# Float32 for the first two blocks, six raw slots and another order of the first steps in a chunked-attention, mixing and FFN kernel

## The chip, the cores and the metric

The kernel runs on one core of a Trainium2 chip. The metric is device time in microseconds of one execution; the median of three runs stands for the kernel. Five engines have queues of their own: TensorE (PE, products; its weight loads are listed as PEld), VectorE (DVE), ScalarE (ACT), GpSimd (POOL) and SyncE (SP, which here issues nearly all transfers).

## The reference

Four batches of 768 tokens, 8 heads of 64. Each chunk of 32 queries sees 16 tokens to its left, itself, 8 to its right and 8 memory tokens. Then a gated mixing and an FFN follow:

```python
scores = scale * np.matmul(q_c, k_full.transpose(0, 1, 3, 2))
scores = scores - np.max(scores, axis=-1, keepdims=True)
a = np.exp(scores); a = a / (np.sum(a, axis=-1, keepdims=True) + 1e-09)
out[:, :, c_start:c_end] = np.matmul(a, v_full)
# mixing, x is the attention's output as (B, S, 512)
gate_pre += conv_w[k][None, None, :] * xp[:, k:k + S, :]      # 5 taps along the tokens
gate = 1.0 / (1.0 + np.exp(-gate_pre))
x = gate * (x @ w_val) @ w_out
# FFN on the normalised x
ch = np.maximum(xn @ w_ch1, 0.0) @ w_ch2                       # 512 -> 2048 -> 512
out = x + ch
```

The weights w_val, conv_w, w_out, w_ch1 and w_ch2 arrive as 64-bit floats, 20 pieces of 1 MB in all (and conv_w).

## The kernel before

**Tiling.** The tokens are cut into 24 sub-blocks of 128 (two pairs of chunks each). Sub-blocks are grouped into 13 blocks: one alone, eleven of two, one alone (lines 222 to 225). Each block goes through attention (`attention`, in 8 steps per sub-block), mixing (`mix`, 8 steps and 2 more per sub-block) and FFN (`ch1` and `ch2`, `finish`).

**Precision.** Nearly every product is made of three float16 products: both operands are scaled by a power of two and split into a high and a low half (`PASSES`, line 36). For the operands of attention, `attention` squares and sums q, k and v on ScalarE (lines 251 to 253), derives the scales with a small product and three integer operations (`totals`, `pow2`), and writes each high half on ScalarE and each low half on VectorE (lines 264 to 278, 320 and 321). The probabilities are turned around by two DMA transposes on SP's queue (line 325). Block 0 alone is mixed and sent through the FFN in float32, with unsplit weights (`split` is false for it); its attention is of the float16 kind.

**Weights.** `fetch` and `take` load a piece of a weight as raw 64-bit words; `to_f32` makes float32 of it with one ScalarE and one VectorE pass (lines 153 and 154). `gram` adds the products of the piece with itself to get a bound for its scale (line 197); ahead of them `fill` issues eight products of the preceding piece into a tile "idle" that nothing reads (lines 177 to 182). When all pieces of a weight are through, `weight_scale` gives its scale, and `split_weight` writes the two halves in place (lines 217 and 218). Raw pieces lie in four slots inside the tile of the second FFN weight, and, from the seventeenth piece on, mostly in two buffers of their own (line 160).

**Order.** Everything is cut into streams of steps: a (attention), x (mixing), f (FFN), w (fetches), m, 1 and 2 (conversion, scale and split of the mixing weights, the first and the second FFN weight), l (loads of q, k, v). The string `PLAN` (line 35) writes out the order of the first 126 steps; then `STEADY` (line 34) is gone through for each block, in which attention runs two blocks and mixing one block ahead of the FFN. The framework turns this order into the queues of the engines and may let an instruction pass another that waits. The loads of a sub-block use buffers that alternate between two (`NLD`).

Of the kernel before, what the change touches and what calls it, by code (L numbers as in the profile page):

```python
# [49 lines left out]
def chunk_attention_moe_kernel(ctx: ExitStack, tc: tile.TileContext,  # L50
# [39 lines left out]
    bd = [const.tile([P, HP, 2, 2, 2, CHUNK], F16, name=f"bd{i}") for i in range(2)]  # L90
# [149 lines left out]

    def attention(n, d, u):
# [51 lines left out]

        sc = at.tile([P, 2 * HP, NSEEN], F32, tag="sc", name="sc")
        by_group = sc.rearrange("p (a g) k -> p a g k", g=2)
        for g in range(2):
            for ch in range(2):
                pp = slice(ch * 64, (ch + 1) * 64)
                nc.scalar.activation(out=by_group[pp, :, g, :],  # L299
                                     in_=s_ps[g][pp, :, ch * CHUNK:ch * CHUNK + NSEEN], func=AF.Copy)  # L300
        wide = [P, 2 * HP, NSEEN]
        mx = sm_p.tile([P, 2 * HP, 1], F32, tag="mx", name="mx")
        nc.vector.tensor_reduce(out=mx, in_=sc, axis=AX.X, op=ALU.max)
        nc.vector.tensor_tensor(out=sc, in0=sc, in1=mx.to_broadcast(wide), op=ALU.subtract)
        nc.scalar.activation(out=sc, in_=sc, func=AF.Exp, scale=c_exp)

        if i == 0:
            nc.vector.memset(by_group[0:64, :, 0, 0:LEFT], 0.0)
        if i == NSUB - 1:
            nc.vector.memset(by_group[64:128, :, 1, NSEEN - RIGHT:NSEEN], 0.0)  # L310
        yield

        sm = sm_p.tile([P, 2 * HP, 1], F32, tag="sum", name="sum")
        rs = sm_p.tile([P, 2 * HP, 1], F32, tag="rs", name="rs")
        nc.vector.tensor_reduce(out=sm, in_=sc, axis=AX.X, op=ALU.add)
        nc.vector.tensor_scalar(out=sm, in0=sm, scalar1=1e-9, scalar2=2.0 ** -PSCALE, op0=ALU.add, op1=ALU.mult)
        nc.vector.reciprocal(out=rs, in_=sm)
        nc.vector.tensor_tensor(out=sc, in0=sc, in1=rs.to_broadcast(wide), op=ALU.mult)  # L318
# [12 lines left out]
        xT = d["xT"][:, :, u, :]  # L331
        if i == 0:
            nc.gpsimd.memset(xT[:, :, 0:KW - 1], 0.0)
        else:
            nc.gpsimd.tensor_copy(out=xT[:, :, 0:KW - 1], in_=tail[0][:, :, SUB:SUB + KW - 1])
        tail[0] = xT
# [10 lines left out]
        for g, t in enumerate(pv):  # L347
            for e in range(2):
                pp = slice(e * 64, (e + 1) * 64)
                o = xT[pp, :, c0 + g * 64:c0 + (g + 1) * 64].rearrange("p a (c q) -> p a c q", q=CHUNK)  # L350
                if e == 0 or n < EVAC_ACT:
                    nc.scalar.activation(out=o, in_=t[pp, :, :, e, :], func=AF.Copy, scale=c_pv[pp])
                else:
                    nc.vector.tensor_scalar(out=o, in0=t[pp, :, :, e, :], scalar1=c_pv[pp], scalar2=None,
                                            op0=ALU.mult)
        if d["split"]:
            xs = xT[:, :, c0:c0 + SUB]
            xh, xl = (t[:, :, off:off + SUB] for t in d["x"])
            nc.scalar.activation(out=xh, in_=xs, func=AF.Copy, scale=s[:, 2:3])  # L359
            nc.vector.scalar_tensor_tensor(out=xl, in0=xs, scalar=s[:, 2:3], in1=xh, op0=ALU.mult, op1=ALU.subtract)  # L360
# [5 lines left out]
    def open_block(j):  # L366
        d = blk[j] = {"T": blocks[j][1] * SUB, "iv": {}, "split": j > 0}
        d["xT"] = x_p.tile([P, HP, 2, KW - 1 + SUB], F32, tag="xT", name="xT")
        if d["split"]:
# [4 lines left out]

    def mix(j):
# [68 lines left out]
        for u in range(n):  # L444
# [255 lines left out]
```

## Time and profile before

| | us |
|---|---|
| median of 3 runs | 766.37 (765.82 to 766.48) |
| the profiled execution | 764.73 |
| its span, first to last instruction | 762.6 |
| PE busy | 724.4 (95%) |
| DVE busy | 529.5 (69%) |
| ACT busy | 423.4 (56%) |
| POOL busy | 8.9 (1%) |

The profile counts an engine as busy while one of its instructions runs; a chain of waits, a table of stages and a timeline can be drawn from the same trace. Because a product's end is modelled and products overlap, the time of a group of products is its busy time divided by their number, not the mean of one.

### The profile page before, as it was taken

What the parts mean: (1) busy time and instruction counts of PE and PEld (TensorE: products, weight loads), DVE (VectorE), ACT (ScalarE), POOL (GpSimd) and SP (SyncE); (2) the same over time, 40 slices, a digit from 0 to 9 for tenths busy, and PEclk for the clock granted to TensorE, in tenths of its full rate; (3) what the DMA queues carried; (4) which work ended last, traced back from release to release, by engine and by line L of the source; (5) the groups of instructions that cost most, each with busy time, mean ns of one, the idle gap of its engine ahead of it and who ended that gap; (6) DMA issues with size and microseconds to landing.
All of it is one profiled execution on the core that took longest, in us unless ns stands there. A gap on an engine that the chain in (4) does not pass through costs nothing.

```text
span 762.6 us, 15675 instructions
## 1 busy us (share of the span) xinstructions
PE 724.4 (95%) x6480; PEld 496.8 (65%) x6480; DVE 529.5 (69%) x1163; ACT 423.4 (56%) x733; POOL 8.9 (1%) x35
## 2 busy tenths in 40 slices
PE   3888988888999999999999999999999999999997
PEld 2457745655766766766766766766767766766675
DVE  5799988885865866866876776776776776662321
ACT  7879968764663663664564565465465464330210
POOL 2000000000000000000000000000000000000000
PEclk9999999999999999999999999999999999999999
DMA  9969433222232132232212223223223102010010
GB/s 355 358 223 341 181 90 91 78 77 70 63 77 71 63 77 70 68 72 70 77 64 70 77 64 81 66 70 82 59 77 91 43 18 53 16 26 30 1 43 15
DMA packets 69735, 68.93 MB, mean 90 GB/s; under 512 B 53280, under 2 KB 53280, under 8 KB 69664
## 3 DMA queue, kind: packets, MB, share of 16 engines
q1 hardware_dynamic: 69376, 67.91, 29.9%
q8 instruction: 51, 0.84, 0.5%
q14 instruction: 20, 0.16, 0.1%
q10 hardware_dynamic: 288, 0.02, 0.0%
HBM read 49.30 MB, written 6.29 MB: 73 GB/s over the span
## 4 chain that ended last, share of the span: by engine, by line
PE 77%; DVE 11%; ACT 7%; DMA 3%; issue 1%; ACTq 0%; DVEq 0%
PE c_ps L477 30%; PE acc L497 29%; PE yps L424 7%; PE val L406 7%; PE s_ps L287 3%; DVE gt L389 2%; PE pv L344 2%; DVE w L154 2%; DMA xn<-xh 1%; ACT bd L268 1%; ACT top L153 1%; DVE w L218 1%; DMA raw<-in_w_ch_dram 1%; ACT sc L299 1%; DMA pT<-p 1%
## 5 line engine op out<-in xcount | busy, mean ns | idle before, releaser
L497 PE MATMUL acc<-w,h 128*128 128x512 f16 (+1 forms) x1136 | 266.2, 385 | 0.0
L477 PE MATMUL c_ps<-xn,w 128*128 128x256 f16 (+1 forms) x2304 | 256.8, 269 | 6.7 <-DMA xn<-xh 6.7
L477 PEld LDWEIGHTS <-w 128*128 128x128 f16 x2304 | 216.1, 98 | 44.6 <-DMA xn<-xh 7.0
L497 PEld LDWEIGHTS <-h 128*128 128x128 f16 x1104 | 107.0, 98 | 114.8 <-DVE h L482 0.2
L480 ACT ACTIVATE h<-c_ps 128x512 f16<-128x512 f32 (+1 forms) x96 | 56.5, 589 | 79.0 <-PE c_ps L477 76.5
L482 DVE SCALAR_TENSOR_TENSOR h<-c_ps,h 128x512 f16<-128x512 f32 x92 | 63.0, 685 | 53.2 <-ACT h L480 53.2
L389 DVE SCALAR_TENSOR_TENSOR gt<-xT,cw_sb,gt 128x256 f32<-128x256 f32 (+1 forms) x208 | 82.4, 458 | 0.1
L424 PE MATMUL yps<-wo,hg 128*128 128x512 f16 x276 | 64.4, 383 | 0.0
L406 PE MATMUL val<-x,wv 128*128 128x256 f16 (+1 forms) x576 | 62.4, 268 | 0.9 <-ACT x L359 0.8
L406 PEld LDWEIGHTS <-wv 128*128 128x128 f16 x576 | 54.4, 98 | 7.3 <-issue 1.2
L299 ACT ACTIVATE sc<-s_ps 64x256 f32<-64x256 f32 x96 | 36.3, 378 | 24.5 <-PE s_ps L287 23.5
L253 ACT ACTIVATE vs<-vt 128x1024 bf16<-128x1024 f32 x24 | 25.1, 1047 | 38.6 <-PE pv L344 38.4
L424 PEld LDWEIGHTS <-hg 128*128 128x128 f16 x276 | 25.9, 98 | 29.1 <-issue 1.0
L457 ACT ACTIVATE xh<-xh 128x512 f16<-128x512 f32 x23 | 14.5, 629 | 47.3 <-DVE xh L446 25.8
L287 PEld LDWEIGHTS <-bd 128*128 128x128 f16 x576 | 28.4, 99 | 17.8 <-issue 13.6
L411 ACT ACTIVATE hg<-gt 128x512 f16<-128x512 f32 (+1 forms) x24 | 14.6, 611 | 44.7 <-DVE gt L408 44.7
L268 ACT ACTIVATE bd<-qt,s 64x512 f16<-64x512 f32 x48 | 34.2, 713 | 7.0 <-DVE s L123 5.6
L269 DVE SCALAR_TENSOR_TENSOR bd<-qt,s,bd 64x512 f16<-64x512 f32 x48 | 35.7, 745 | 2.0 <-ACT bd L268 0.7
L287 PE MATMUL s_ps<-ks,bd 128*128 128x96 f16 x576 | 30.2, 209 | 6.6 <-ACT ks L271 5.3
L458 DVE TENSOR_TENSOR xh<-xh,xh 128x512 f16<-128x512 f32 x23 | 15.9, 692 | 29.4 <-DMA xn<-xh 22.8
L504 DVE SCALAR_TENSOR_TENSOR y<-acc,co_w,y 128x512 f32<-128x512 f32 x23 | 16.2, 746 | 28.4 <-PE acc L497 28.4
L320 ACT ACTIVATE p<-sc 128x512 f16<-128x512 f32 x24 | 15.1, 627 | 37.4 <-DVE sc L318 37.4
(120 smaller groups left out, 778.2 us busy)
## 6 DMA issues: line engine op xcount, KB each, us to landing
vt<-in_v_dram SPq DMA_DIRECT2D x24, 512.0 KB, 4.3
kt<-in_k_dram SPq DMA_DIRECT2D x24, 384.0 KB, 3.7
w<-in_w_ch_dram SPq DMA_DIRECT2D x8, 1023.8 KB, 8.0
qt<-in_q_dram SPq DMA_DIRECT2D x24, 256.0 KB, 2.7
out_dram<-y SPq DMA_DIRECT2D x24, 256.0 KB, 2.1
w<-in_w_ch_dram SPq DMA_DIRECT2D x5, 1023.5 KB, 6.5
raw<-in_w_ch_dram SPq DMA_DIRECT2D x3, 1023.5 KB, 12.5
w<-in_w_val_dram SPq DMA_DIRECT2D x2, 1023.5 KB, 7.5
```

The costliest lines, as they stand in the source:

```text
L253: nc.scalar.activation(out=v2[0].bitcast(BF16), in_=vt, func=AF.Square, accum_out=ss[:, 2:3])
L268: nc.scalar.activation(out=hi, in_=src, func=AF.Copy, scale=s[pp, 0:1])
L269: nc.vector.scalar_tensor_tensor(out=lo, in0=src, scalar=s[pp, 0:1], in1=hi, op0=ALU.mult, op1=ALU.subtract)
L287: nc.tensor.matmul(out=t[:, hp, :], lhsT=bd[r0][:, hp, g].rearrange("p c e q -> p (c e q)"), rhs=k2[r1][:, hp, g, :], start=(x == 0), stop ...
L299: nc.scalar.activation(out=by_group[pp, :, g, :], in_=s_ps[g][pp, :, ch * CHUNK:ch * CHUNK + NSEEN], func=AF.Copy)
L389: nc.vector.scalar_tensor_tensor(out=o, in0=xT[:, hp, 0:n, kk:kk + SUB], scalar=cw_sb[:, kk, hp:hp + 1], in1=o, op0=ALU.mult, op1=ALU.add)
L406: nc.tensor.matmul(out=t[:, u, 0:T], lhsT=l, rhs=r, start=(x == 0), stop=(x == len(todo) - 1))
L424: nc.tensor.matmul(out=t, lhsT=l, rhs=r, start=(x == 0), stop=(x == len(todo) - 1))
L477: nc.tensor.matmul(out=t[:, u * T:(u + 1) * T], lhsT=l, rhs=r, start=(x == 0), stop=(x == len(todo) - 1))
L480: nc.scalar.activation(out=h[0], in_=t, func=AF.Relu)
L482: nc.vector.scalar_tensor_tensor(out=h[1], in0=t, scalar=0.0, in1=h[0], op0=ALU.max, op1=ALU.subtract)
L497: nc.tensor.matmul(out=a, lhsT=l, rhs=r, start=(m == 0 and x == 0), stop=(m == NM - 1 and x == len(todo) - 1))
```

## The change

- Attention of the first two blocks (three sub-blocks) goes through a new function `attention32`: the queries are copied unscaled into a float32 view of the tile that held both halves, the products take q, k, v and the probabilities in float32, and the probabilities are turned around by products with a unit matrix and moved out of PSUM by VectorE. It has 5 steps per sub-block. The tile of the queries is zeroed again before the first float16 attention.
- Mixing of both blocks is float32; the FFN is so for block 0 alone, as before.
- Raw pieces use six slots from the start: four in the second FFN weight's tile and two buffers.
- `fill` and its products go.
- `PLAN` is another order of 120 steps. A conversion whose piece has not been asked for asks for it.

The diff, without the code that only moved into `exponentials`, `normalize`, `place` and `activations`:

```diff
-NFILL = 8
+NF32 = 2
+FIRST = 1
-PLAN = "w2 a1 w2 a2 m2 w1 l1 a1 w1 m2 a4 m1 a1 w2 x2 1_1 x2 w1 1_2 w1 l1 1_1 w1 a2 1_1 w1 x1 a1 w1 x1 1_1 a1 x3 a1 1_1 a3 m4 a2 x1 1_1 2_1 a1 w1 1_1 w2 2_2 a1 2_1 w1 2_1 a1 w1 a2 2_1 x2 w1 x2 w1 x1 l1 x1 f2 x1 f1 x1 2_1 1_1 2_1 a4 f2 x3 2_1 f1 1_1 f1 2_1 f1 2_2 l1 2_2 1_6 2_1 x1 2_2 f1"
+PLAN = "l1 a2 w1 a1 w1 m1 a2 x2 m1 w2 x2 w1 m1 a3 w2 l1 w2 x1 m1 w1 x1 w1 x3 m1 1_2 a2 1_3 x1 1_1 w1 1_1 a2 w1 a3 x3 w1 x2 1_1 x2 m2 f1 w1 2_1 x1 f1 1_1 w1 2_1 x1 l1 x1 2_1 a2 x1 1_2 2_1 x1 a1 2_1 a1 2_2 1_1 2_1 f2 1_1 m1 w1 f1 l1 a1 l1 2_1 a1 1_1 f1 1_1 w1 f1 1_1 2_1 f2 2_4 a1 2_1 f1 2_1 1_1 2_1 m1"
...
-    bd = [const.tile([P, HP, 2, 2, 2, CHUNK], F16, name=f"bd{i}") for i in range(2)]
+    bdt = const.tile([P, 2, HP, 2, 2, 2, CHUNK], F16, name="bd")
+    bd = [bdt[:, r] for r in range(2)]
+    bd32 = bdt.rearrange("p r a g c e q -> p (r a g c e q)").bitcast(F32).rearrange(
+        "p (a g c e q) -> p a g c e q", a=HP, g=2, c=2, e=2)
...
-        at = 4 * (n % 4) + 1 if n < 16 else 13 if n == 18 else None
+        at = ([1, 5, 9, 13, None, None] * 2 + [1, 5, 9, 13, None, None, 13, None])[n]
...
-    idle = [None]
-
-    def fill(n):
-        if idle[0] is not None:
-            t = ps_c.tile([P, 512], F32, tag="c", name="idle")
-            for _ in range(n):
-                nc.tensor.matmul(out=t, lhsT=idle[0][:, 0:P], rhs=idle[0][:, 0:512], start=True, stop=True)
-        idle[0] = None
...
-        fill(NFILL)
-        if W is not W2:
-            idle[0] = w[:, :, 1]
...
+    first16 = sum(sizes[:NF32])
...
+    def attention32(n, d, u):
         b, i = divmod(n, NSUB)
         st = sub[n]
         qt, kt, vt = st["q"], st["k"], st["v"]
+        for e in range(2):
+            pp = slice(e * 64, (e + 1) * 64)
+            src = qt[pp].rearrange("p a (n q) -> p (a n) q", q=CHUNK)
+            dst = bd32[pp, :, :, :, e, :].rearrange("p a g c q -> p (a g c) q")
+            if e == 0:
+                nc.scalar.activation(out=dst, in_=src, func=AF.Copy)
+            else:
+                nc.vector.tensor_copy(out=dst, in_=src)
+        yield
+        s_ps = []
+        for g in range(2):
+            t = ps.tile([P, HP, KEYS], F32, tag="ps", name="s_ps")
+            for hp in range(HP):
+                nc.tensor.matmul(out=t[:, hp, :], lhsT=bd32[:, hp, g].rearrange("p c e q -> p (c e q)"),
+                                 rhs=kt[:, hp, g, :], start=True, stop=True)
+            s_ps.append(t)
+        yield
+        sc, by_group = exponentials(i, s_ps, float(D) ** -0.5)
+        yield
+        normalize(sc, 1.0)
+        t = ps.tile([P, HP, P], F32, tag="ps", name="pT_ps")
+        for hp in range(HP):
+            nc.tensor.matmul(out=t[:, hp, :], lhsT=sc[:, 2 * hp:2 * hp + 2, :].rearrange("p g k -> p (g k)"), rhs=eye,
+                             start=True, stop=True)
+        pT = at.tile([P, 2, HP, P], F16, tag="pT", name="pT").rearrange("p r a t -> p (r a t)").bitcast(F32)
+        pT = pT.rearrange("p (a t) -> p a t", a=HP)
+        nc.vector.tensor_copy(out=pT, in_=t)
+        yield
+        xT = place(d, u, i)
+        pv = [ps.tile([P, HP, 2, 2, CHUNK], F32, tag="ps", name="pv") for g in range(2)]
+        for hp in range(HP):
+            for ch in range(2):
+                for g in range(2):
+                    pp = slice(g * 64, (g + 1) * 64)
+                    nc.tensor.matmul(out=pv[g][:, hp, ch].rearrange("p e q -> p (e q)"),
+                                     lhsT=vt[pp, ch, hp * P:(hp + 1) * P], rhs=pT[pp, hp, ch * 64:(ch + 1) * 64],
+                                     start=True, stop=True)
+        activations(n, xT, pv, 1.0)
+        yield
+
+    def attention(n, d, u):
...
+        if d["f32"]:
+            yield from attention32(n, d, u)
+            return
+        if n == first16:
+            nc.gpsimd.memset(bdt, 0.0)
...
-        d = blk[j] = {"T": blocks[j][1] * SUB, "iv": {}, "split": j > 0}
+        d = blk[j] = {"T": blocks[j][1] * SUB, "iv": {}, "split": j > 0, "f32": j < NF32}
...
-        split = d["split"]
+        split = not d["f32"]
...
-                todo = [p for kc in range(KC) for p in passes(Wv.rows(kc, split, fc * P, P), [x[:, kc, 0:T] for x in d["x"]])]
+                todo = [p for kc in range(KC) for p in passes(Wv.rows(kc, split, fc * P, P), [x[:, kc, 0:T] for x in d["x"]]
+                                                           if split else [xT[:, kc, 0:n, KW - 1:KW - 1 + SUB]])]
...
-        for t in tops + bd + [eye]:
+        for t in (tops[0], bdt, *tops[1:], eye):
             nc.gpsimd.memset(t, 0.0)
...
             for jj in range(W.n):
+                while jj not in W.raw:
+                    next(streams["w"])
                 convert(W, jj)
...
-        per = {"a": lambda n: 8 * n, "x": lambda n: 8 + 2 * n, "f": lambda n: NM * n * SUB // 256}
+        per = {"a": lambda j, n: (5 if j < NF32 else 8) * n, "x": lambda j, n: 8 + 2 * n, "f": lambda j, n: NM * n * SUB // 256}
```

## Rows read from the trace of the kernel before

**Rows 1.** Engine totals of the page: busy time, share of the span, instructions.
```profile
PE 724.4 (95%) x6480; PEld 496.8 (65%) x6480; DVE 529.5 (69%) x1163; ACT 423.4 (56%) x733; POOL 8.9 (1%) x35
```
**Rows 2.** Stages: window, its length, then each engine's busy time; last columns named by the first line.
```profile
core 0: us, PE busy (x) PEld busy (x) DVE busy (x) ACT busy (x) POOL busy (x), PEclk, DMA share, GB/s
0.00:65.00 65.00, 45.40 (x423) 27.79 (x424) 50.56 (x111) 54.40 (x81) 4.99 (x14) 1.00 0.87 322
65.00:117.00 52.00, 46.43 (x413) 33.54 (x413) 48.97 (x103) 42.49 (x63) 0.31 (x2) 1.00 0.52 173
117.00:191.00 74.00, 64.90 (x604) 44.40 (x605) 57.52 (x114) 48.40 (x84) 0.59 (x3) 0.95 0.28 76
191.00:700.00 509.00, 509.00 (x4534) 351.12 (x4532) 357.87 (x805) 270.00 (x493) 2.97 (x16) 1.00 0.24 63
700.00:762.60 62.60, 58.65 (x514) 39.94 (x512) 14.54 (x32) 8.12 (x14) 0.00 (x0) 1.00 0.06 18
```
**Rows 3.** The same table for line 181 alone, first stage: PE, PEld, clock, DMA.
```profile
0.00:65.00 65.00, 24.29 (x96) 8.91 (x96) 1.00 0.87 322
```
**Rows 4.** Timeline of TensorE: start, duration, line, operation, count, idle before and its releaser.
```profile
13.86 1.03 PE L197 MATMUL gram<-wv 128*128 128x128 bf16 x8 [0.58 <-DVE wv L154]
17.00 0.62 PE L197 MATMUL gram<-wv 128*128 128x128 bf16 x8
...
64.77 3.17 PE L477 MATMUL c_ps<-xnf,w 128*128 128x128 f32 x26 [1.40 <-DVE xnf L452]
...
161.44 0.20 PE L344 MATMUL pv<-pT,vs 64*128 64x64 f16 x2 [2.05 <-DMA pT<-p]
```
**Rows 5.** Groups by form, 0 to 190 us, VectorE: busy, mean ns, idle before.
```profile
L154 DVE SCALAR_TENSOR_TENSOR w<-w,top 128x1024 int32<-128x1024 int32 x13 | 15.8, 1217 | 1.8 <-ACT top L153 1.8
L389 DVE SCALAR_TENSOR_TENSOR gt<-xT,cw_sb,gt 128x256 f32<-128x256 f32 x32 | 13.2, 475 | 0.0
L269 DVE SCALAR_TENSOR_TENSOR bd<-qt,s,bd 64x512 f16<-64x512 f32 x14 | 10.5, 747 | 1.5 <-ACT bd L268 0.7 <-issue 0.5
L277 DVE SCALAR_TENSOR_TENSOR vs<-vt,s,vs 128x1024 f16<-128x1024 f32 x7 | 9.0, 1283 | 0.4 <-ACT vs L276 0.4
L272 DVE SCALAR_TENSOR_TENSOR ks<-kt,s,ks 128x768 f16<-128x768 f32 x7 | 7.1, 1017 | 0.5 <-ACT ks L271 0.3
L321 DVE TENSOR_TENSOR p<-sc,p 128x512 f16<-128x512 f32 x7 | 4.8, 687 | 0.0
L360 DVE SCALAR_TENSOR_TENSOR x<-xT,s,x 128x512 f16<-128x512 f32 x5 | 3.7, 748 | 1.5 <-ACT x L359 1.5
L446 DVE TENSOR_SCALAR xh<-y,mv,rt 128x512 f32<-128x512 f32 x5 | 2.7, 546 | 0.2
L452 DVE TENSOR_TENSOR xnf<-xnT,g_sb 128x512 f32<-128x512 f32 x1 | 0.7, 684 | 0.0
```
**Rows 6.** The same view, ScalarE.
```profile
L253 ACT ACTIVATE vs<-vt 128x1024 bf16<-128x1024 f32 x9 | 9.4, 1047 | 2.6 <-PE pv L344 2.4 <-DMA vt<-in_v_dram 0.3
L276 ACT ACTIVATE vs<-vt,s 128x1024 f16<-128x1024 f32 x7 | 8.0, 1137 | 0.0
```
**Rows 7.** The same view, TensorE.
```profile
L477 PE MATMUL c_ps<-xnf,w 128*128 128x128 f32 x128 | 16.2, 279 | 1.4 <-DVE xnf L452 1.4
L497 PE MATMUL acc<-w,h 128*128 128x512 f32 x32 | 14.3, 595 | 0.0
L424 PE MATMUL yps<-wo,hg 128*128 128x512 f16 x48 | 12.1, 401 | 0.0
L406 PE MATMUL val<-x,wv 128*128 128x256 f16 x96 | 11.0, 272 | 0.9 <-ACT x L359 0.8
```
**Rows 8.** Timeline of TensorE, one sub-block's score and value products.
```profile
167.81 1.18 PE L287 MATMUL s_ps<-ks,bd 128*128 128x96 f16 x24
...
184.52 0.87 PE L344 MATMUL pv<-pT,vs 64*128 64x64 f16 x48
```
**Rows 9.** Chain that ended last, in order of time: start, duration, what.
```profile
75.30 5.62 DMA raw<-in_w_ch_dram
```
**Rows 10.** Stages as in rows 2, around one pause.
```profile
160.00:170.00 10.00, 8.23 (x95) 4.80 (x96) 8.86 (x18) 7.81 (x14) 0.00 (x0) 0.83 0.45 104
```

More of the change, by code (lines that the diff above doesn't have):

```diff
@@ new lines, in normalize, with place @@
+    def normalize(sc, by):
+        sm = sm_p.tile([P, 2 * HP, 1], F32, tag="sum", name="sum")
+        rs = sm_p.tile([P, 2 * HP, 1], F32, tag="rs", name="rs")
+        nc.vector.tensor_reduce(out=sm, in_=sc, axis=AX.X, op=ALU.add)
+        nc.vector.tensor_scalar(out=sm, in0=sm, scalar1=1e-9, scalar2=by, op0=ALU.add, op1=ALU.mult)
+        nc.vector.reciprocal(out=rs, in_=sm)
+        nc.vector.tensor_tensor(out=sc, in0=sc, in1=rs.to_broadcast(WIDE), op=ALU.mult)
+    def place(d, u, i):
+        xT = d["xT"][:, :, u, :]
+        if i == 0:
+            nc.gpsimd.memset(xT[:, :, 0:KW - 1], 0.0)
+        else:
+            nc.gpsimd.tensor_copy(out=xT[:, :, 0:KW - 1], in_=tail[0][:, :, SUB:SUB + KW - 1])
+        tail[0] = xT
+        return xT
@@ new lines, in activations @@
+    def activations(n, xT, pv, c_pv):
+        c0 = KW - 1
+        for g, t in enumerate(pv):
+            for e in range(2):
+                pp = slice(e * 64, (e + 1) * 64)
+                o = xT[pp, :, c0 + g * 64:c0 + (g + 1) * 64].rearrange("p a (c q) -> p a c q", q=CHUNK)
+                if e == 0 or n < EVAC_ACT:
+                    nc.scalar.activation(out=o, in_=t[pp, :, :, e, :], func=AF.Copy, scale=c_pv if isinstance(c_pv, float) else c_pv[pp])
+                else:
+                    nc.vector.tensor_scalar(out=o, in0=t[pp, :, :, e, :], scalar1=c_pv if isinstance(c_pv, float) else c_pv[pp], scalar2=None,
+                                            op0=ALU.mult)
@@ new lines, in attention32 @@
+    def attention32(n, d, u):
+        b, i = divmod(n, NSUB)
+        st = sub[n]
+        qt, kt, vt = st["q"], st["k"], st["v"]
+        for e in range(2):
+            pp = slice(e * 64, (e + 1) * 64)
+            src = qt[pp].rearrange("p a (n q) -> p (a n) q", q=CHUNK)
+            dst = bd32[pp, :, :, :, e, :].rearrange("p a g c q -> p (a g c) q")
+            if e == 0:
+                nc.scalar.activation(out=dst, in_=src, func=AF.Copy)
+            else:
+                nc.vector.tensor_copy(out=dst, in_=src)
[22 more added lines that the diff above has]
+        for hp in range(HP):
+            for ch in range(2):
+                for g in range(2):
+                    pp = slice(g * 64, (g + 1) * 64)
[4 more added lines that the diff above has]
+        yield
@@ L291, in attention @@
         yield
[L294 to L310, printed above, removed]
-        yield
[L313 to L318, printed above, removed]
+        sc, by_group = exponentials(i, s_ps, c_exp)
+        yield
+        normalize(sc, 2.0 ** -PSCALE)
         p2 = [at.tile([P, 2 * HP, NSEEN], F16, tag=f"p{r}", name=f"p{r}") for r in range(2)]
@@ L329, in attention @@
         yield
[L331 to L336, printed above, removed]
+        xT = place(d, u, i)
         c0, off = KW - 1, u * SUB
@@ L346, in attention @@
                                          rhs=pT[r1][pp, hp, ch * 64:(ch + 1) * 64], start=(x == 0), stop=(x == 2))
[L347 to L360, printed above, removed]
+        activations(n, xT, pv, c_pv)
+        xs = xT[:, :, c0:c0 + SUB]
+        xh, xl = (t[:, :, off:off + SUB] for t in d["x"])
+        nc.scalar.activation(out=xh, in_=xs, func=AF.Copy, scale=s[:, 2:3])
+        nc.vector.scalar_tensor_tensor(out=xl, in0=xs, scalar=s[:, 2:3], in1=xh, op0=ALU.mult, op1=ALU.subtract)
         yield
@@ L366, in open_block @@
     def open_block(j):
-        d = blk[j] = {"T": blocks[j][1] * SUB, "iv": {}, "split": j > 0}
+        d = blk[j] = {"T": blocks[j][1] * SUB, "iv": {}, "split": j > 0, "f32": j < NF32}
         d["xT"] = x_p.tile([P, HP, 2, KW - 1 + SUB], F32, tag="xT", name="xT")
-        if d["split"]:
+        if not d["f32"]:
             d["x"] = [x_p.tile([P, HP, 2 * SUB], F16, tag=f"x{r}", name=f"x{r}") for r in range(2)]
-        else:
-            d["x"] = [d["xT"][:, :, 0, KW - 1:]]
         return d
@@ L416, in mix @@
         y = d["y"] = y_p.tile([P, 2, DM], F32, tag="y", name="y")
-        xn = d["xn"] = [xn_p.tile([P, KC, 2 * SUB], F16, tag=f"xn{r}", name=f"xn{r}") for r in range(2)] if split else \
+        xn = d["xn"] = [xn_p.tile([P, KC, 2 * SUB], F16, tag=f"xn{r}", name=f"xn{r}") for r in range(2)] if d["split"] else \
             [b_p.tile([P, KC, 2 * SUB], F16, tag="hg0", name="xnf").rearrange("p k t -> p (k t)").bitcast(F32).rearrange("p (k t) -> p k t", t=SUB)]
@@ L447, in mix @@
                                     op0=ALU.subtract, op1=ALU.mult)
-            if not split:
+            if not d["split"]:
                 t = ps.tile([P, KC, P], F32, tag="ps", name="xnT")
@@ L637, in chunk_attention_moe_kernel @@
             count[c] += 1
-        per = {"a": lambda n: 8 * n, "x": lambda n: 8 + 2 * n, "f": lambda n: NM * n * SUB // 256}
+        per = {"a": lambda j, n: (5 if j < NF32 else 8) * n, "x": lambda j, n: 8 + 2 * n, "f": lambda j, n: NM * n * SUB // 256}
         ahead = {"f": 0, "x": 1, "a": 2}
         for j in range(NB):
-            limit = {c: sum(per[c](n) for _, n in blocks[:j + a + 1]) for c, a in ahead.items()}
+            limit = {c: sum(per[c](i, n) for i, (_, n) in enumerate(blocks[:j + a + 1])) for c, a in ahead.items()}
             for c in expand(STEADY):
```

24 lines of the change are left out of this document (20 added, 4 removed).

## The prediction, made before the changed kernel was run

> **What bounds the kernel now.** I read the engine totals first, then the table by stages, then single rows of the start. TensorE is busy 724.4 of 762.6 us [rows 1], and the stage table shows that from 191 to 700 us it never pauses: that stretch is products alone, and nothing of it is touched except what has been done before it [rows 2]. So everything is decided in the first 191 us and, unchanged, in the tail. In the stages TensorE is idle 19.6 us of the first 65, 5.6 of the next 52, 9.1 of the next 74 and 3.9 in the tail: 38.2 in all [rows 2]. Of its busy time in the first stage 24.3 us are the products into "idle" that nothing reads [rows 3]. Without them the first stage holds 45.4 - 24.3 = 21.1 us of wanted work, and 43.9 us are empty. The whole account is 700.1 us wanted work + 24.3 filler + 38.2 idle.
>
> Why is the first stage empty? The first FFN product of block 0 starts at 64.77 us, released by VectorE [rows 4]. Till then VectorE is busy 50.6 of 65 us and ScalarE 54.4, while the DMA engines are at 0.87 [rows 2]. They convert weights, split queries, keys and values into two halves, and mix block 0. This conveyor, not TensorE, sets the start. After 65 us TensorE is busy near nine tenths of the time and its gaps are short waits on VectorE's and the transposes' chains.
>
> **The change, part by part.** The sum is made on the profiled execution: its span is 762.6 us, the execution is 764.73 (2.1 around the span), and the median of the three runs is 766.37, 1.6 more. So span + 3.8 is what I forecast for the median.
>
> *Products that nothing reads.* 96 products go, 24.3 us of busy TensorE. Nobody reads them; an instruction behind them waits at most one set of eight, 2.0 us. I cost their removal at no gain of its own, because TensorE is not what the first stage waits for. [...]
>
> *Attention of three sub-blocks in float32 (block 0 has one, block 1 two).* On VectorE each sub-block loses two low halves of the queries (2 x 0.747), those of the keys (1.017), the values (1.283) and the probabilities (0.687), 4.48 us [rows 5]. It gains one copy of half the queries, which the trace does not show; the nearest row of one source and float32 in and out is the normalisation, 0.546 [rows 5], for all 128 partitions, and I take that (bounds 0.3 and 0.75). It also gains one move of the transposed probabilities out of PSUM, 0.684 by the row of the same size [rows 5]. Net 3.25 us, for three 9.75. Two sub-blocks also lose the low half of the mixed input (0.748 each [rows 5]): 11.2 us, a floor, since ten tiny scale instructions each go too. ScalarE loses at least the large Square (1.047) and the value split (1.137) [rows 6] and some five more passes, well over 10 us for three; it stops being the second limit.
> On TensorE, float32 costs more. Busy time by count: a float32 record takes 16.2/128 = 0.127 us at 128 columns and 14.3/32 = 0.447 at 512, two records a product [rows 7]; between them about 0.23 at 256 and 0.10 at 96 (estimates on the straight line through these two). Scores: 16 records, 1.6 to 2.0 us, for 1.18 [rows 8]. Transposing by products: 8 records, 1.0, new; it takes the place of two DMA transposes. Second product: 32 records of 64 columns on half the rows, 1.2 (halves side by side) to 2.3, for 0.87 [rows 8]. So +1.7 to +3.2 each; I take 2.2, in the middle, and 6.5 for three (5 to 9.6).
>
> *Mixing of block 1 in float32.* Value product: 32 records of 0.23, 7.4 us, for 48 at 11.0/96 = 0.114, 5.5 [rows 7]. Output product: 16 of 0.447, 7.2, for 24 at 0.22, 5.2 (12.1/48 = 0.25 with its gaps [rows 7]). Together +4. In all wanted work becomes 700.1 + 6.5 + 4 = 710.6, at most 714. VectorE and ScalarE lose the two splits of the gated values (not counted above). The four pieces of the mixing weights no longer have to be split before block 1, only before block 2: work moved, not removed.
>
> *Six raw slots.* At the start six pieces instead of four are asked for. In the first 40 us the DMA engines are full anyway, so there it brings nothing; it can close the holes after. What it can win is seen in the last piece: asked for at 75.3 us, landed 5.6 later, with the chain to block 1 standing on it [rows 9].
>
> *New order of the first steps.* Block 1's attention and most of its mixing move ahead of the first FFN step of block 0; weight conversions of the second FFN matrix and the splits move behind. With it go the loads: sub-block 2's values now wait until the float32 product of sub-block 0 has read the same buffer, and on SP's queue the weight pieces behind them wait along. At most two pieces' fetch lies in that shadow; with seven pieces already asked for I cost it at nothing, and at up to 3 us (a piece of 1 MB at the first stage's 322 GB/s [rows 2]) if that cover is gone. The zeroing of the query tiles for the later float16 attention goes to GpSimd between sub-blocks 2 and 3; that engine is idle, and nobody needs it before three ScalarE passes later: nothing, at most 2.
>
> *The sum.* VectorE's work ahead of the first FFN step stays about the same: savings of some 8.5 us for two and a half attentions and two conversions less (2 x 1.22 [rows 5]), against block 1's taps and gates (16 x 0.41 to 0.475 [rows 5] and 1.3) and the rest of sub-block 2, together near 11. So 50.6 us again. At the density of before (50.6 of 65) the step starts at 65; if VectorE were as full as it is in the second stage (48.97 of 52 [rows 2]) at 54. With ScalarE relieved and the pieces earlier I take 60. By then TensorE has done 21.1 + 0.9 (third sub-block's second product) + 6.5 + 7.4 = 36 us, not 21.1. Left: 710.6 - 36 = 674.6. Later idle: the 5.6 of the second stage end in the wait for block 1's transposes, whose chain now starts much earlier, so I halve them; 9.1 and 3.9 stay: 15.8. Span 60 + 674.6 + 15.8 = 750.4, forecast **754.2 us**.
>
> **The rivals.** *1. The clock (slower).* [...] Chance 0.17.
> [...]
>
> *2. More gain.* If VectorE is the limit up to block 2, its 157.05 us before 191 [rows 2] become at most 145.8; at the same density (0.82) that is 177 us, 14 earlier, and with the uncounted splits and scales 19 earlier: **747 to 752**, or 741 where the first FFN step comes at 54 and half of the later idle goes. Against it: TensorE would have to be 0.9 busy from the first products on. Chance below 748: 0.25.
>
> *3. No gain.* The order on an engine is not the written order alone (splits of the first FFN matrix run in the trace before pieces that are written ahead of them), so the first FFN step may stay where it is, at 65, float32 costs 714, and the chain from the last piece [rows 9] still ends at 118 us: 65 + 678 + 18.6 = 761.6 span, **765 us**. For it speaks that the DMA engines are already full in the first 40 us. Chance 0.13. That the written order doesn't come about falls under it.
>
> **How the numbers follow.** Forecast 754 (748 to 760) 0.45, more gain 0.25, no gain 0.13, slower 0.17. A difference of 0.2% (1.5 us) is about what a measurement can tell from none. Half of "no gain" lies below 764.8: faster 0.76, same 0.06, slower 0.18. The range leaves out the better end of rival 2 and the worse half of rival 1: 742 to 769.
>
> **What would show it.** Right: no rows into "idle"; the first FFN product near 60 us; TensorE's wanted work before it near 36 us; no pause of several us before block 1's first FFN step; the stretch without pause beginning near 180 us. Wrong: a granted clock well under 1 in the first 70 us with Gram sets of 1 us each (rival 1); the first FFN product still at 65 us, or the last piece landing after 80 (rival 3); float32 scores over 2 us a sub-block.

## The result and the profile after

The changed kernel takes 754.63 us (median of 4 runs, 753.84 to 756.27) against 766.21 for the kernel before: ratio 0.9852, 95% interval 0.9835 to 0.9869. A second measurement, beside the last experiments, gave 754.28 us, ratio 0.9829 (0.9812 to 0.9846). The forecast was 754.2. The gain is some 12 us, and all of it lies before the stretch in which TensorE never pauses.

The engine totals of the page after, to be read beside [rows 1]:

```profile
span 752.7 us, 15260 instructions
PE 720.5 (96%) x6309; PEld 503.9 (67%) x6309; DVE 515.0 (68%) x1133; ACT 401.9 (53%) x699; POOL 10.9 (1%) x35
```

The same stages as [rows 2], after (window, its length, busy time of each engine, granted clock, DMA share, GB/s):

```profile
0.00:65.00 65.00, 51.35 (x407) 46.36 (x408) 44.06 (x104) 38.11 (x58) 7.36 (x16) 1.00 0.88 348
65.00:117.00 52.00, 46.67 (x345) 29.70 (x346) 47.40 (x87) 43.57 (x60) 0.00 (x0) 0.97 0.42 136
117.00:191.00 74.00, 64.56 (x587) 43.48 (x585) 60.71 (x128) 48.51 (x87) 0.59 (x3) 0.95 0.29 77
191.00:700.00 509.00, 509.00 (x4530) 350.90 (x4529) 349.63 (x787) 264.76 (x484) 2.98 (x16) 1.00 0.24 62
700.00:752.70 52.70, 48.89 (x448) 33.49 (x446) 13.16 (x30) 6.93 (x12) 0.00 (x0) 1.00 0.07 21
```

In the first 65 us TensorE is busy 51.4 us, and every product is wanted; before it was 45.4, of which 24.3 were filler [rows 2, 3]. VectorE and ScalarE have become emptier there (50.6 to 44.1 and 54.4 to 38.1 us). The two later stages look as before: 5.3 and 9.4 us idle.

TensorE's timeline after shows where the time came from (start, duration, line, count, idle before and its releaser; line 301 is the float32 scores, 310 the transposing products, 322 the float32 value products, 188 the Gram products, 461 the mixing's value product, 532 the FFN's first product):

```profile
5.76 3.73 PE L301 MATMUL s_ps<-kt,bd 128*128 128x96 f32 x16 [5.76 <-ACT bd L293]
14.68 2.05 PE L310 MATMUL pT_ps<-eye,sc 128*128 128x128 f32 x8 [5.19 <-DVE sc L259]
16.52 1.06 PE L188 MATMUL gram<-wv 128*128 128x128 bf16 x8
17.51 3.68 PE L322 MATMUL pv<-pT,vt 64*128 64x64 f32 x32
21.12 1.17 PE L301 MATMUL s_ps<-kt,bd 128*128 128x96 f32 x4
22.08 1.06 PE L188 MATMUL gram<-wv 128*128 128x128 bf16 x8
22.94 2.81 PE L301 MATMUL s_ps<-kt,bd 128*128 128x96 f32 x12
...
37.91 1.13 PE L310 MATMUL pT_ps<-eye,sc 128*128 128x128 f32 x8 [1.02 <-DVE va L491]
39.90 2.00 PE L322 MATMUL pv<-pT,vt 64*128 64x64 f32 x32
43.42 1.92 PE L301 MATMUL s_ps<-kt,bd 128*128 128x96 f32 x16
45.18 1.53 PE L532 MATMUL c_ps<-xnf,w 128*128 128x128 f32 x12
...
56.91 7.07 PE L461 MATMUL val<-xT,wv 128*128 128x256 f32 x32
...
82.58 1.12 PE L532 MATMUL c_ps<-xnf,w 128*128 128x128 f32 x8
...
101.81 0.38 PE L532 MATMUL c_ps<-xn,w 128*128 128x256 f16 x2 [0.17 <-DMA xn<-xh]
...
104.40 0.28 PE L532 MATMUL c_ps<-xn,w 128*128 128x256 f16 x1 [0.99 <-DMA xn<-xh]
...
104.55 6.74 PE L532 MATMUL c_ps<-xn,w 128*128 128x256 f16 x45
...
175.13 0.37 PE L532 MATMUL c_ps<-xn,w 128*128 128x256 f16 x1 [3.15 <-DMA xn<-xh]
176.54 4.75 PE L532 MATMUL c_ps<-xn,w 128*128 128x256 f16 x23 [1.04 <-DMA xn<-xh]
```

The first FFN product of block 0 comes at 45.2 us, not 64.8 [rows 4], and its 128 records stretch to 83.7 with block 1's mixing between them. Block 1's FFN begins in earnest at 104.6; before, the same products began at 118.3:

```profile
116.91 0.39 PE L477 MATMUL c_ps<-xn,w 128*128 128x256 f16 x2 [2.97 <-DMA xn<-xh]
118.30 5.14 PE L477 MATMUL c_ps<-xn,w 128*128 128x256 f16 x31 [0.99 <-DMA xn<-xh]
...
188.36 2.69 PE L477 MATMUL c_ps<-xn,w 128*128 128x256 f16 x23 [2.49 <-DMA xn<-xh]
```

The stretch without pause begins at 176.5 us after and at 188.4 before (last row): 11.8 us earlier, while the span is 9.9 shorter in these two executions and the medians differ by 11.6. The 1.9 us between are lost at once: the first 23 products of the stretch take 4.75 us after and 2.69 before. The granted clock of the ten microseconds around them is 0.70 after and 1.00 before (first row after, second row before, columns of [rows 2]):

```profile
170.00:180.00 10.00, 5.81 (x72) 3.68 (x71) 3.06 (x6) 3.11 (x6) 0.20 (x1) 0.70 0.42 107
180.00:190.00 10.00, 7.30 (x86) 4.20 (x84) 4.60 (x8) 3.53 (x7) 0.20 (x1) 1.00 0.41 107
```

### The profile page after: what moved, and what is told of

Read it like the earlier page. It is cut to its first block, busy times and chain, and to the rows that moved or that the text cites. A ratio compares the mean times of both kernels' runs of the same rounds, so it can differ in the third digit from the quotient of the medians.

```text
span 752.7 us, 15260 instructions
## 1 busy us (share of the span) xinstructions
PE 720.5 (96%) x6309; PEld 503.9 (67%) x6309; DVE 515.0 (68%) x1133; ACT 401.9 (53%) x699; POOL 10.9 (1%) x35
## 4 chain that ended last, share of the span: by engine, by line
PE 77%; ACT 6%; DVE 4%; DMA 2%; issue 1%; SPq 0%; DVEq 0%; ACTq 0%
PE c_ps L532 31%; PE acc L552 29%; PE val L461 7%; PE yps L479 7%; PE s_ps L379 2%; PE pv L409 2%; DMA xn<-xh 1%; ACT top L158 1%; DVE w L209 1%; DVE gt L443 1%; ACT w L208 1%; ACT sc L240 1%; ACT bd L360 1%; ACT ks L363 0%; ACT vs L345 0%
## 5 line engine op out<-in xcount | busy, mean ns | idle before, releaser
L532 PE MATMUL c_ps<-xn,w 128*128 128x256 f16 (+1 forms) x2304 | 259.5, 270 | 5.3 <-DMA xn<-xh 5.3
L532 PEld LDWEIGHTS <-w 128*128 128x128 f16 x2304 | 217.3, 99 | 45.4 <-issue 5.4
L479 PE MATMUL yps<-wo,hg 128*128 128x512 f16 x252 | 58.0, 379 | 0.0
L461 PE MATMUL val<-x,wv 128*128 128x256 f16 (+1 forms) x528 | 56.9, 268 | 0.0
L461 PEld LDWEIGHTS <-wv 128*128 128x128 f16 x528 | 49.7, 98 | 5.5
L345 ACT ACTIVATE vs<-vt 128x1024 bf16<-128x1024 f32 x21 | 22.0, 1046 | 36.5 <-PE pv L409 36.5
L479 PEld LDWEIGHTS <-hg 128*128 128x128 f16 x252 | 23.4, 98 | 26.1
L512 ACT ACTIVATE xh<-xh 128x512 f16<-128x512 f32 x23 | 14.5, 629 | 44.1 <-DVE xh L501 22.1
L466 ACT ACTIVATE hg<-gt 128x512 f16<-128x512 f32 (+1 forms) x22 | 13.4, 610 | 45.2 <-DVE gt L463 45.2
L361 DVE SCALAR_TENSOR_TENSOR bd<-qt,s,bd 64x512 f16<-64x512 f32 x42 | 31.2, 743 | 1.4 <-ACT bd L360 0.7
L360 ACT ACTIVATE bd<-qt,s 64x512 f16<-64x512 f32 x42 | 29.9, 713 | 3.4 <-DVE s L128 2.9
L280 DVE TENSOR_SCALAR xT<-pv,c_pv 64x256 f32<-64x256 f32 x42 | 18.8, 489 | 17.3 <-ACT xT L278 17.1
L463 DVE SCALAR_TENSOR_TENSOR gt<-gt,val 128x512 f32<-128x512 f32 (+1 forms) x26 | 16.6, 646 | 16.2 <-PE val L461 15.7
```

The lines of the kernel that those rows point to most:

```text
L345: nc.scalar.activation(out=v2[0].bitcast(BF16), in_=vt, func=AF.Square, accum_out=ss[:, 2:3])
L360: nc.scalar.activation(out=hi, in_=src, func=AF.Copy, scale=s[pp, 0:1])
L361: nc.vector.scalar_tensor_tensor(out=lo, in0=src, scalar=s[pp, 0:1], in1=hi, op0=ALU.mult, op1=ALU.subtract)
L461: nc.tensor.matmul(out=t[:, u, 0:T], lhsT=l, rhs=r, start=(x == 0), stop=(x == len(todo) - 1))
L479: nc.tensor.matmul(out=t, lhsT=l, rhs=r, start=(x == 0), stop=(x == len(todo) - 1))
L532: nc.tensor.matmul(out=t[:, u * T:(u + 1) * T], lhsT=l, rhs=r, start=(x == 0), stop=(x == len(todo) - 1))
```

## The experiments

My theory: float32 takes work off VectorE, which sets the start, and lets block 1's attention and mixing run before the FFN; filler, slots and clock hardly matter. The rivals: the filler's removal is the gain; the filler held the clock up; the order alone is the gain; ScalarE, not VectorE, is what was relieved; the pieces' arrival sets the start. Ratios are against the kernel before, run beside each; differences to the changed kernel are given against its 0.9852 and 0.9829 (754.6 and 754.3 us).

**The filler, taken from the kernel before.**

```diff
-        fill(NFILL)
```

> The kernel before without the 96 filler products, nothing else. Theory (TensorE is not what the first 65 us wait for): 766 us, within 1.5 of before; the Gram sets of the first 60 us take up to 1.06 us instead of 0.62, and the first FFN product stays within 1.5 us of 64.8. Rival A (the filler is 24 us of TensorE in the way, its removal is the gain): 755 to 760. Rival B (the filler holds the clock up and pays for itself): 770 or more.

770.01 us, ratio 1.0048 (1.0030 to 1.0066): 3.7 us slower. That is rival B's figure, at its edge. The first stage of its table and the stage from 191 to 700 us, in the columns of [rows 2], and from its timeline the first FFN product, the set that before started at 188.36, and one later pause:

```profile
0.00:65.00 65.00, 32.25 (x321) 25.51 (x322) 49.41 (x109) 53.09 (x79) 4.99 (x14) 0.75 0.85 312
191.00:700.00 509.00, 506.00 (x4508) 348.20 (x4506) 356.94 (x804) 269.57 (x493) 2.97 (x16) 1.00 0.25 63
```
```profile
66.96 3.17 PE L476 MATMUL c_ps<-xnf,w 128*128 128x128 f32 x26 [0.78 <-DVE xnf L451]
...
189.65 2.69 PE L476 MATMUL c_ps<-xn,w 128*128 128x256 f16 x23 [0.95 <-DMA xn<-xh]
...
414.57 2.33 PE L496 MATMUL acc<-w,h 128*128 128x512 f16 x10 [1.25 <-DVE h L481]
```

The granted clock of the first 65 us falls from 1.00 to 0.75, the wanted work takes 32.3 us instead of 21.1, and the first FFN product comes 2.2 us later. In the kernel before the filler was no waste; it bought the clock. But the clock of the start is not shown to cost all of the 3.7 us. In the traced execution, 5.4 us longer in span than that of the kernel before, the delay is 1.3 us at the stretch without pause (189.65 for 188.36); most of the rest comes behind 240 us, where TensorE pauses five times for 3.0 us in all, which the kernel before does not. Why these pauses come with the filler gone, no run shows.

**The filler, put back into the changed kernel.**

```diff
+        fill(NFILL)
+        if W is not W2:
+            idle[0] = w[:, :, 1]
```

> The changed kernel with the filler of before put back at the same Gram steps. Theory (filler and clock hardly matter): 755 to 758, a little over the changed kernel's 754.6, since TensorE now has only 13.7 us idle in the first 65 and the 24 us of filler don't all fit. Rival A (filler in the way): 765 and more. Rival B (the clock lost in the first 30 us costs the gain of the filler): 750 to 752.

770.26 us, ratio 1.0044 (1.0030 to 1.0058): 15.6 us slower than the changed kernel (14.7 to 16.5 by the ratios). Rival A, in this kernel. Its first stage, and where its first FFN product and block 1's FFN begin:

```profile
0.00:65.00 65.00, 53.48 (x377) 38.76 (x384) 36.36 (x84) 35.13 (x50) 7.05 (x14) 1.00 0.92 364
```
```profile
62.61 3.79 PE L545 MATMUL c_ps<-xnf,w 128*128 128x128 f32 x32
...
118.08 5.40 PE L545 MATMUL c_ps<-xn,w 128*128 128x256 f16 x48
```

The clock column stays at 1.00 and the first FFN product still comes 17.4 us later: TensorE, which with the filler pauses less than 1 us between 14.5 and 65 us, is now the engine that is short, and the Gram sets with their filler stand in its queue ahead of the wanted products. VectorE does less by 65 us (36.4 against 44.1), because it waits. (The framework orders its queues anew with the filler in, so not all 15.6 us are the filler's own duration.) So taking the 96 products out of the one kernel costs 3.7 us, and putting them into the other costs 15.6.

**Four raw slots in the changed kernel.**

```diff
-        at = ([1, 5, 9, 13, None, None] * 2 + [1, 5, 9, 13, None, None, 13, None])[n]
+        at = 4 * (n % 4) + 1 if n < 16 else 13 if n == 18 else None
```

> The changed kernel with the four raw slots of before. Theory (the DMA engines are full in the first 40 us anyway): 755 to 757, the last piece landing some 2 us later. Rival (the pieces' arrival sets the start): 760 and more, with conversions that wait for a piece.

767.83 us, ratio 1.0014 (0.9998 to 1.0030), and it says nothing on the slots. In the new order a fifth and sixth piece are asked for before the first is converted, so with four slots raw pieces are overwritten before their conversion; the weights that this kernel computes with are others, and each early conversion waits for a piece fetched four later. This account is argued from the order and not shown; so what late pieces would cost stays open, and all that the run says is that this order can't do with the four slots as they stand.

**Float16 attention in the new order.** The eight steps of the old attention are drawn together into five; mixing of block 1 stays float32.

```diff
+            if d["f32"]:
+                g = attention(first + u, d, u)
+                for k in (2, 1, 1, 3, 1):
+                    for _ in range(k):
+                        next(g, None)
+                    yield
```

> The changed kernel, its order kept, with the float16 attention of before in the first three sub-blocks (its eight steps drawn together into five); mixing of both blocks stays float32. Theory (VectorE's and ScalarE's relief is most of the gain): 762 to 766, VectorE's busy time before 65 us not lower but block 1's first FFN product (104.5 us in the changed kernel) 8 us or more later. Rival (the order, with mixing ahead of the FFN, makes the gain): 755 to 757.

773.92 us, ratio 1.0093 (1.0076 to 1.0110): 19.3 us more than the changed kernel (18.5 to 20.2 by the ratios), and more than the kernel before. Beyond the theory's figure, far from the rival's. Its first stage:

```profile
0.00:65.00 65.00, 35.39 (x365) 28.98 (x365) 46.28 (x103) 50.88 (x77) 5.01 (x13) 0.92 0.87 331
```
```profile
57.45 2.72 PE L530 MATMUL c_ps<-xnf,w 128*128 128x128 f32 x22 [0.32 <-DVE xnf L505]
...
119.63 0.24 PE L404 MATMUL pv<-pT,vs 64*128 64x64 f16 x2 [7.64 <-DMA pT<-p]
```

ScalarE is back at 50.9 us, and a single wait for the DMA transposes of a sub-block's probabilities holds TensorE up for 7.64 us. The order alone, as it was run here, gains nothing; drawing eight steps into five may have a part in that wait, which no run tells apart.

**Float32 in the old order.** The kernel before without filler, with the new attention and mixing; the attention's five steps stand where the old ones stood, and the splits of the mixing weights go to the end of the written order.

```diff
-PLAN = "... 1_1 a3 m4 a2 x1 ... x1 2_2 f1"
+PLAN = "... 1_1 a3 a2 x1 ... x1 2_2 f1 m4"
```

> The kernel before without filler, with the float32 attention and mixing of the first two blocks, but in the order of before (the steps of the new attention stand where those of the old stood; the splits of the mixing weights go behind block 1's mixing) and with four raw slots. Without filler alone it was 770.0. Theory (float32 relieves VectorE and ScalarE whatever the order): 760 to 765, a third to two thirds of the way from 770.0 to 754.6. Rival (float32 pays only together with the new order, as the new order paid nothing with float16 attention, 773.9): 768 to 772.

764.43 us, ratio 0.9986 (0.9970 to 1.0002); without filler alone the ratio was 1.0048. So float32 is worth about 4.8 us in the old order by the totals (0.0062 of 767). At the theory's upper edge. Its first products of the two FFN blocks:

```profile
57.87 2.94 PE L545 MATMUL c_ps<-xnf,w 128*128 128x128 f32 x24 [1.25 <-DVE xnf L520]
...
125.79 7.64 PE L545 MATMUL c_ps<-xn,w 128*128 128x256 f16 x48 [6.28 <-DMA xn<-xh]
```

The first comes 9.1 us earlier than without filler alone (66.96), but block 1's come 4.9 us later (125.8 for 120.9), after a wait of 6.28 us for transposes: what float32 gains at the front, the old order loses again before block 1.

**The same with six slots.**

```diff
-        at = 4 * (n % 4) + 1 if n < 16 else 13 if n == 18 else None
+        at = ([1, 5, 9, 13, None, None] * 2 + [1, 5, 9, 13, None, None, 13, None])[n]
```

> The precision part in the order of before without filler (764.4 with four slots), now with the six raw slots. Theory (the DMA engines are full in the first 40 us, so slots alone bring little): 763 to 765; the ten us to the changed kernel are then the order's. Rival (six slots are what lets the pieces come while float32 frees the engines): 756 to 760.

765.13 us, ratio 0.9971 (0.9954 to 0.9988), which overlaps four slots' interval. In the old order slots bring nothing that can be told. In this run's trace the set of 23 products that opens the stretch without pause starts at 188.92 us, 0.7 earlier than without filler alone (189.65), and no pause follows; so most of float32's 4.8 us in the old order lies in the late pauses of that other run, which are not explained. From here to the changed kernel (0.9829 on the same chip) only the order is left: 0.0142, 10.9 us.

**Useless passes back on ScalarE.** Five per float32 sub-block:

```diff
+        nc.scalar.activation(out=k2[1]..., in_=qt..., func=AF.Square, accum_out=ss[:, 0:1])
+        nc.scalar.activation(out=k2[0].bitcast(BF16), in_=kt, func=AF.Square, accum_out=ss[:, 1:2])
+        nc.scalar.activation(out=v2[0].bitcast(BF16), in_=vt, func=AF.Square, accum_out=ss[:, 2:3])
+        nc.scalar.activation(out=k2[0], in_=kt, func=AF.Copy)
+        nc.scalar.activation(out=v2[0], in_=vt, func=AF.Copy)
```

> The changed kernel with five useless passes put back on ScalarE for each of the three float32 sub-blocks (three Squares, two conversions of keys and values), some 5.1 us each, 15.4 in all. Theory (ScalarE is not the limit once relieved: 38.1 of 65 us busy): 754.6 to 757. Rival (ScalarE's relief is the gain, since the conversions begin there): 762 and more.

762.33 us, ratio 0.9948 (0.9930 to 0.9966): 7.4 to 9.1 us slower than the changed kernel for 15.4 us of work. That is the rival's figure; the theory fell here. The passes stand at the head of each sub-block's attention, and the first scores come 3.6 us later for it (9.34 us for 5.76); what the same passes would cost elsewhere, no run shows.

**Useless passes back on VectorE.** Three per float32 sub-block:

```diff
+        nc.vector.scalar_tensor_tensor(out=k2[1], in0=kt, scalar=1.0, in1=kt, op0=ALU.mult, op1=ALU.subtract)
+        for r in range(2):
+            nc.vector.scalar_tensor_tensor(out=v2[r], in0=vt, scalar=1.0, in1=vt, op0=ALU.mult, op1=ALU.subtract)
```

> The changed kernel with three useless passes put back on VectorE for each of the three float32 sub-blocks (one over the keys, two over the values), 3.6 us each, 10.7 in all: about what float32 took off VectorE. Theory (VectorE sets the start): 760 to 765, most of the 10.7 coming back as time. Rival (VectorE has room in the first 65 us, 44.1 busy, and the gain is ScalarE's or the order's): 754.6 to 757.

759.61 us, ratio 0.9910 (0.9890 to 0.9930): 4.5 to 6.2 us for 10.7 us of work. Just under the theory's range. The first stage of the two, ScalarE's first:

```profile
0.00:65.00 65.00, 46.77 (x354) 41.50 (x355) 37.00 (x86) 46.04 (x75) 7.05 (x14) 0.92 0.85 329
```
```profile
0.00:65.00 65.00, 46.20 (x383) 41.19 (x384) 48.46 (x100) 35.11 (x52) 7.81 (x14) 0.89 0.89 349
```

In both TensorE has done some 5 us less by 65 us (2.7 and 3.2 less than the 49.4 in the second measurement of the changed kernel), though neither engine is full, and the first FFN product comes at 54.6 and 53.0 us for 45.2. A us on either costs about half a us (7.4/15.4 = 0.48, 4.5/10.7 = 0.42, and 0.59 and 0.58 against the second measurement). I read the start as a relay between the two, not one engine's queue.

**Block 1's mixing in float16 products.** Attention stays float32; the mixed input gets a constant scale, and the splits of the mixing weights move ahead of it.

```diff
+        if not d["mix32"]:
+            nc.scalar.activation(out=xh, in_=xs, func=AF.Copy, scale=2.0 ** 14)
+            nc.vector.scalar_tensor_tensor(out=xl, in0=xs, scalar=2.0 ** 14, in1=xh, op0=ALU.mult, op1=ALU.subtract)
```

> The changed kernel with block 1's mixing in float16 products (attention stays float32, with a constant scale for the mixed input), the four splits of the mixing weights moved ahead of it. Theory, with what useless passes cost (about 0.45 us per us on VectorE or ScalarE): some 8 us more on VectorE and 7 on ScalarE before block 1, 4 less on TensorE: 757 to 760. Rival (mixing in float32 pays nothing, its dearer products eat the relief): 753 to 755.5.

759.45 us, ratio 0.9898 (0.9882 to 0.9915), against 0.9829 for the changed kernel beside it: 5.3 us, the moved splits included. As the theory had it.

**Unread products ahead of the first scores.**

```diff
+    def warm():
+        for n in (45, 90):
+            t = ps_c.tile([P, 512], F32, tag="c", name="warm")
+            for _ in range(n):
+                nc.tensor.matmul(out=t[:, 0:P], lhsT=ones, rhs=ones, start=True, stop=True)
+            yield
```

> The changed kernel with products of a tile of ones on TensorE while it waits at the start: 45 of 128 columns before the first scores and 90 between them and the transposing products, so that the first sub-block's products run at the full clock (scores 1.92 us for 16 records instead of 3.73, value products 2.0 instead of 3.68). Theory A (the low clock of the first 25 us lies on the first block's chain): 750 to 752.5, the first FFN product 2 to 4 us earlier. Theory B (pieces and VectorE set the start, the clock costs latency that something else covers): within 1 us of 754.6.

757.50 us, ratio 0.9889 (0.9867 to 0.9911). Its timeline:

```profile
5.63 2.02 PE L308 MATMUL s_ps<-kt,bd 128*128 128x96 f32 x16
...
42.31 3.50 PE L308 MATMUL s_ps<-kt,bd 128*128 128x96 f32 x16
45.65 1.30 PE L539 MATMUL c_ps<-xnf,w 128*128 128x128 f32 x10
...
178.28 0.59 PE L539 MATMUL c_ps<-xn,w 128*128 128x256 f16 x2 [5.99 <-DMA xn<-xh]
```

The first scores take 2.02 us, as meant, but then TensorE waits for VectorE's conversions (1.75 and 1.10 us before 25.3 and 27.0), slows again (scores 3.50 us at 42.3; granted clock 0.90 from 30 to 65 us), and the first FFN product comes at 45.65, no earlier. Theory B on this point. The 2.8 us or more that are lost come later: block 1's FFN begins at 102.3 us, 2.2 earlier than in the changed kernel, but before 178.3 TensorE waits 5.99 us for block 2's transposes, where the changed kernel waits 3.15. Why, I did not test (the order that the framework made differs there).

**Products in the waits for the transposes.**

```diff
+            if j == 2 or (j == 1 and u == n - 1):
+                t = ps_c.tile([P, 512], F32, tag="c", name="bridge")
+                for _ in range(7):
+                    nc.tensor.matmul(out=t, lhsT=x2[0][:, 0:P], rhs=x2[0], start=True, stop=True)
```

> The changed kernel with seven products of the normalised rows' high half, which nothing reads, issued on TensorE while it waits for the DMA transposes of block 1's second and block 2's two sub-blocks. In the changed kernel it pauses there (3.15 and 1.04 us before 175 and 176.5) and the next 23 products take 4.75 us, not 2.7. Theory (from here on TensorE is what everything waits for, so its clock is time): 751.5 to 753.5. Rival (the seven products delay the first real ones as much as the clock gives back): 754.5 to 757.

770.68 us, ratio 1.0043 (1.0029 to 1.0057): 16 us slower, which neither had. The timeline shows where most of it arises:

```profile
86.28 0.63 PE L188 MATMUL gram<-w 128*128 128x128 bf16 x8 [0.21 <-DVE w L159]
90.25 0.63 PE L188 MATMUL gram<-w 128*128 128x128 bf16 x8 [3.34 <-DVE w L159]
92.13 1.04 PE L188 MATMUL gram<-w 128*128 128x128 bf16 x8 [1.25 <-DVE w L159]
95.42 1.03 PE L188 MATMUL gram<-w 128*128 128x128 bf16 x8 [2.25 <-DVE w L159]
98.98 3.02 PE L519 MATMUL bridge<-xh 128*128 128x512 f16 x7 [2.53 <-ACT xh L512]
101.83 7.31 PE L536 MATMUL c_ps<-xnf,w 128*128 128x128 f32 x64
```

The extra products stand in TensorE's queue ahead of half of block 0's first FFN products. Those 64 records, which in the changed kernel fill the gaps between the Gram sets and are through by 83.7 us, now start at 101.8, and block 1's FFN begins at 116.0 us for 104.6, 11.4 of the 14.6 us by which this execution's span is longer. What the clock costs at 175 us is not settled by this run; the result's two timelines put it at some 2 us (4.75 for 2.69, at a granted clock of 0.70 for 1.00).

## Why the prediction was right, and where it was not

*The time.* 754.2 forecast, 754.6 measured, but its terms were wrong by 8 to 15 us and cancelled; that the two figures agree to 0.4 us is luck. The sum had 710.6 us of wanted work and 39.8 idle (24 before the first FFN step, 15.8 later); the execution has 720.5 busy and 32.2 idle (13.7 in the first 65 us, then 5.3, 9.4 and 3.8). In the sum's own terms: the first FFN product at 45.2 us for 60 (-14.8); by then 31.6 us of work done for 36, so 688.9 left for 674.6 (+14.3); 18.6 us idle after it for 15.8 (+2.8). That makes a span of 752.7 for 750.4, and the 3.8 us added to the span for the median were 1.9. Part of the cancelling has a reason: where TensorE waits anyway, a product that takes longer fills a gap, so that busy time grows and idle time shrinks. With the first scores at 2.02 us instead of 3.73, behind unread products, the first FFN product came no earlier (45.65 us for 45.2).

*Wanted work, 9.9 us too low.* The slow products of the first 25 us account for some 5.9 us. First scores 3.73 for 1.92, transposing products 2.05 for 1.13, value products 3.68 for 2.00, two Gram sets 1.06 for 0.62, and the second sub-block's scores 3.98 (1.17 and 2.81) for 1.92: 1.81 + 0.92 + 1.68 + 0.88 + 2.06 = 7.4, of which some 1.5 was in the 700.1 already, since the kernel before too took 2.24 us for its first scores (later 1.18) and 1.03 for its first Gram set. None of it was in the forecast. Another 2.1 us are the 23 products after the pause at 175 us. Then comes the price of float32 attention: 1.92 + 1.13 + 2.00 = 5.05 us a sub-block for 2.05 [rows 8], so +3.0 and not the +2.2 I took (the bounds held), 2.4 for three. The mixing's value product was near, 7.07 us for a forecast of 7.4, but the whole of block 1's mixing went up by 2.6 us and not by 4 (14.6 for 12.0 by busy time, since its float16 output product had taken 6.4 and not 5.2). Together that is 9.0 of the 9.9. By these traces a float32 product of 256 columns took 3.9 times as long as a float16 one: 7.07 us for 16 (in 32 records) against 5.40 for 48.

*The first FFN product at 60 us.* Wrong: 45.2. I followed the written order, in which the step stands behind most of block 1's mixing; in the trace it stands ahead of block 1's value product (45.2 and 56.9 us), so the framework had moved it forward. I had used just this behaviour in rival 3, and only against the change.

*The second stage's gaps halved.* Wrong: 5.3 us for 5.6. The wait for block 1's transposes moved forward by 14 us and did shrink, from 4.0 us (2.97 and 0.99) to 1.2 (0.17 and 0.99), but others took its place in that stage: Gram sets for VectorE (0.95 and 0.84), scores for ScalarE (0.59 and 0.87), value products for their own transposes (0.91). That the third stage's gaps stay was right: 9.4 us for 9.1.

*Filler at nothing, since TensorE is not what is waited for.* Wrong in both kernels: taking it out cost the one 3.7 us (1.3 of it shown at the start), and leaving it in would have cost the other 15.6. The first rival, the clock, had a chance of 0.17 and the upper end of the range, 769; no run shows such a price for the changed kernel, which took 754.6 us. What the runs showed in its place is a granted clock of 0.75 for 1.00 in the first 65 us of the kernel before without filler, where the time rose by 3.7 us. In the changed kernel the Gram sets take 0.62 to 0.64 us from 30.0 us on; in its second traced execution another slow stretch follows, with a Gram set of 1.03 us at 28.9, and the first FFN product comes at 45.5 all the same.

*VectorE sets the start, ScalarE stops being a limit.* Half right. VectorE's savings count (4.5 to 6.2 us for 10.7 put back), but ScalarE's count as much per us (7.4 to 9.1 for 15.4). From 70 to 94 us the chain that ends last is almost wholly ScalarE's; this is part of it, from the changed kernel (start, duration, what):

```profile
80.48 1.04 ACT w L208
81.52 1.26 ACT top L158
...
96.40 2.42 DMA xn<-xh
```

*Six slots nothing.* Right in the old order: no difference that can be told, and the DMA share of the kernel before is 0.98 in the first 40 us. The new order needs them, though.

*Order.* The prediction gave it no term of its own. It is worth 10.9 us with float32 and nothing with float16 attention; float32 is worth 4.8 us by the totals in the old order (0.7 at the start of the stretch without pause) and 19.3 (attention alone) in the new. Neither half would have shown its worth alone.

## What to carry to other kernels

Time an ordering and the work it orders together: here each alone gave 5 us or less, and both 15. In the kernel before, the unread products paid while TensorE had holes in the places where they stood (without them the granted clock of the first 65 us was 0.75 for 1.00, and the time 3.7 us longer); in the changed kernel they did not even in the holes (135 of them in the first 13 us gained nothing), and where wanted work had filled the holes, or the unread ones waited for a late input, they blocked the queue (15.6 and 16 us slower). When two engines hand work to each other, put the work back on each in turn before naming one of them the bottleneck.

## What the runs showed of the hardware that I had not expected

In the first 25 us of the changed kernel TensorE's products took 1.7 to 2.1 times as long as the same products later (float32 scores 3.73 us, later 1.92; Gram sets 1.06, later 0.62), while the clock column says 1.00 there; in this stretch the duration of a known set tells more than the column. With unread products ahead of them the first scores took 2.02 us. That the clock was low there is my reading of these durations; no view shows it. The slow stretch is not the same in every execution of one kernel. In the second traced one the first scores took 3.73 us again, but the first value products, 3.68 us in the execution above, took 2.19:

```profile
17.34 2.19 PE L322 MATMUL pv<-pT,vt 64*128 64x64 f32 x32
```

And products that wait on TensorE held up what stood behind them: from 86 to 99 us it sat idle for 9.6 us in five waits, four before Gram sets and 2.5 us before the seven unread products, while 64 products of block 0's FFN, which the changed kernel had finished by 83.7 us, started only at 101.8, at least 18 us later.
